# Small halves last in the matmuls of h, x2p and o, and a list schedule with other costs for transfers, the shared port and the clock

## The chip, the core and the metric

The kernel runs on one core of a Trainium2 chip, as one program. TensorE (PE) multiplies, VectorE (DVE), ScalarE (ACT) and GpSimd (POOL) work on tiles in SBUF and PSUM, and SyncE (SP) issues most transfers. The metric is the time of one execution in microseconds on the device; the median of three runs of the kernel before is 2260.31 us (2255.88 to 2264.96).

## What is computed

```python
# 4 batches, 8 heads, 768 steps, head 48
k_n = k / (norm(k) + 1e-6)
for t in range(768):
    y[t]  = q[t] @ state
    v_old = state^T k_n[t]
    state = state + beta[t] * outer(k_n[t], v[t] - v_old)
x = y as 3072 tokens of 384 numbers
# dense layer: 384 -> 2048 -> 384
h = x @ w_in;  x = (h * sigmoid(h)) @ w_out
# eight experts of 384 -> 1024 -> 384, all of them for all tokens
P = exp(x @ w_gate - max), normalised 8 times over rows and over columns
out = sum over e of P[:, e] * (relu(x @ w1[e]) @ w2[e])
```

All is float32. The matrix multiplier takes a rounded type (fp32r), so each operand of a large product is split into a large half (the rounded number, "hi") and a small half (what rounding left, "lo"). Each product is three matmuls: hi with hi, hi with lo, lo with hi.

## The kernel before

**Two phases.** Up to about 743 us of the trace the recurrence and the dense layer run side by side; from there to the end the experts run. The recurrence is done in 12 steps of 64 tokens (s = 0 to 11). For a pair of steps, `tri(j)` inverts small triangular matrices column by column on DVE (L540 to L568, the scaling of `nu` at L545, the column operations at L553 and L555). The result goes out to HBM (`rd`) and comes back in another layout (`rt`, L595), and the PE group `z` (L614) of the step waits for that. After z follow on PE r (L627), c (L646), d (L665), y (L680), s (L696), t (L713) and, after the dense layer, l (L831); all of these are narrow matmuls of 16 to 64 columns. `gkq` (L405) makes products of keys ahead of a step. On DVE, `xs` (L701) updates the state.

**The dense layer** works on 6 blocks of 512 tokens (b = 0 to 5; two steps each) and 16 slices f of the hidden size. An `h` operation of the schedule, H(b,f) below, is 9 matmuls into one PSUM bank (L740: 3 row groups k, 3 halves each), then ACT takes the sigmoid (L746), DVE multiplies (`sg`, L750), ACT rounds to the hi half of `g` (L754) and POOL subtracts to get its lo half (L758). An `x2p` operation, X(b,f), is 9 matmuls (L782) of `g` with `w_out`, into three banks `x2p_0` to `x2p_2` that gather over f. In both, the three halves of one k or one bank follow each other. In the first block the weights are split as well: ACT takes absolute values (`wt`, L873) and the hi half (L891), and DVE makes the small half `w` in seven operations (L894 to L905).

**The experts** run in 64 rounds n, in two halves of 32 (of 1536 tokens each). A round has 15 `p` operations (L1213, products of a scheme that saves multiplications; 3 matmuls each) and 12 `o` operations (L1300; 6 matmuls each, for two f; `o{n}_{j}_{i}`). DVE adds the products up (L1022, `s`) and adds `o` to `acc` (L1316); the first copies from PSUM to `s` are ACT's (`evac`, L1227). A finished sum becomes a hidden half in `hidden` (L1239): ACT takes relu into the hi half (L1244) and in place (L1246), and POOL subtracts for the lo half (L1022; tiles `room` or `h`). POOL makes the lo halves of the expert weights (`wa` and `wb`) and the sums of weights (`wraw`).

**What sets the order.** The class `Order` is a list scheduler that runs while the kernel is built. Each operation is put in with its engine, a cost in us, what it depends on (with an offset where one is given), a priority and the buffers that it takes. `emit` simulates the engines with these costs and lets each engine take, among the operations that can start soonest, the one of highest priority; the sequence that comes out is the order of instructions of each engine. The simulation has a model of the PE clock (`pe`, with TICK, PHASE and FULL), in which an operation costs 1.85 times as much where the stretch before had too few columns. An operation marked `port=True` waits for the other of DVE and POOL where that one is also marked; the sums and splits of the experts are not marked. A transfer ends at max(t + 1.5, queue) + cost. While the pipeline fills, `idle` matmuls (L1402) stand in PE's gaps.

Of the kernel before, what the change touches and what calls it, by code (L numbers as in the profile page):

```python
# [24 lines left out]
KD = DM // 128  # L25
# [18 lines left out]
HALVES = ((slice(0, 64), 1), (slice(64, 128), 2))  # L44
NEAR_PE = 0.16
# [11 lines left out]
class Order:  # L57


    QUEUES = ("SP",)  # L60
    LAT = {"PE": 0.2, "ACT": 0.16, "DVE": 0.14, "POOL": 0.1, "SP": 0.08}
# [7 lines left out]
    TICK, PHASE, FULL = 10.24 / 3, 2.63, 2000  # L69

    def add(self, engine, cost, fn, deps=(), prio=1.5, take=(), turn=None, cols=768, port=False):

        d = [x if isinstance(x, tuple) else (x, None) for x in deps]
        self.ops.append((engine, cost, fn, d, prio, take, turn, cols, port))
        return len(self.ops) - 1
# [47 lines left out]
    def pe(self, t, cost, cols):  # L123

        left = 1.0
        while left > 1e-6:
            k = int((t - self.PHASE) / self.TICK + 1 + 1e-6)
            c = cost if self.cols.get(k - 1, 0) >= self.FULL else 1.85 * cost
# [4 lines left out]

    def emit(self, idle=None):
        self.cols, busy = {}, False
# [7 lines left out]
        while any(left.values()):  # L143
            best = None
            for e, todo in left.items():
                c = []
                for i in todo[:WINDOW]:
                    r = None if wait[i] else self.ready(i, end)
                    if r is not None:
                        lane = lanes[-8] + 0.1 if e in self.QUEUES and len(lanes) >= 8 else 0.0  # L150
                        c.append((max(r, now[e], lane, port["POOL" if e == "DVE" else "DVE"] if self.ops[i][8] else 0.0), i))
# [8 lines left out]
                t, i = min((x for x in c if x[0] <= t0 + self.NEAR[e]), key=rank)  # L160
                if best is None or t < best[0]:
                    best = (t, i, e)
            t, i, e = best
# [12 lines left out]
            if e in self.QUEUES:  # L176
                now[e], queue = t + 0.5, max(t + 1.5, queue) + cost
                end[i] = queue
                lanes.append(queue)
            else:  # L180
                if e == "PE":
                    busy = busy or cols == 4608
                    now[e] = max(now[e], IDLE)
                    while idle and not busy and t > IDLE and now[e] + 0.5 < t:
                        order.append((now[e], len(order), None))
                        now[e] = self.pe(now[e], 0.107, 256)
                    t = max(t, now[e])
                    narrow = turn == 1 and cols != 150
# [4 lines left out]
                else:  # L193
                    now[e] = end[i] = t + cost
                    if self.ops[i][8]:
                        port[e] = end[i]
# [10 lines left out]
def kernel(  # L207
# [115 lines left out]
    def load(s, bp, prio):  # L323
# [5 lines left out]
        def gq(p, blk):  # L329
# [3 lines left out]
                op("SP", 0.5, lambda p=p, b=b: gq(p, b), free + [O["gd", s, bp]], prio=prio - 0.1) for p, b in HALVES]  # L333

    def load_part(s, bp, part, prio):
# [4 lines left out]
        if s and not part:  # L340

            return [(op("ACT", 0.45, adma(t(a, 0), kq[s, bp, 0, :, 0]), prio=prio), 2.3),
                    (op("ACT", 0.45, adma(t(b, 0), kq[s, bp, 1, :, 0]), prio=prio), 2.3)]
        return [op("SP", 0.42, dma(t(a, part), kq[s, bp, 0, :, part]), after, prio=prio),
                op("SP", 0.42, dma(t(b, 2 * part), kq[s, bp, 1, :, part]), after, prio=prio)]
# [19 lines left out]
    def gram_k(s, bp):  # L365
# [30 lines left out]
    def gram_kq(s, bp):  # L396
# [20 lines left out]
        q = op("PE", 1.07, lambda: pe(1), ld, prio=prio, take=["a"], turn=1, cols=1088)  # L417
        m = [op("PE", 1.07, lambda: pe(0), ld + [(q, 0.0)], prio=prio, take=["a"], turn=1, cols=1088), q]
        w = []
        for k in range(2):  # L420
# [3 lines left out]
            w.append(op("SP", 0.65, lambda k=k: put(k), [e] + ([(O["nd", s][0], -9.0)] if bp and not k else []), prio=3 - 0.1 * k))  # L424
# [1026 lines left out]
```

## Time and profile before

| what | value |
|---|---|
| median of three runs | 2260.31 us (2255.88 to 2264.96) |
| the profiled execution | 2263.14 us |
| its span in the trace | 2261.4 us |
| PE busy | 2184.4 us, 97% of the span |
| DVE, POOL, ACT busy | 78%, 68%, 45% |

The span is what the profile shows from the first to the last instruction; 1.7 us lie around it. Busy shares are means over stages with different limits, so the rows further down are read by stage: 0 to 106 us fills the pipeline, 106 to 262 us is the first dense block, 262 to 743 us the other five, 743 to 822 us the start of the experts, 1480 to 1540 us their change to the second half of the tokens. "Granted clock" is the share of full speed that TensorE had; its two levels are 2.4 and 1.2 GHz. A wait row says which engine and line sat idle until what, how long in total, how many times and the longest.

### The profile page before, as it was taken

What the parts mean: (1) busy time and instruction counts of PE and PEld (TensorE: products, weight loads), DVE (VectorE), ACT (ScalarE), POOL (GpSimd) and SP (SyncE); (2) the same over time, 40 slices, a digit from 0 to 9 for tenths busy, and PEclk for the clock granted to TensorE, in tenths of its full rate; (3) what the DMA queues carried; (4) which work ended last, traced back from release to release, by engine and by line L of the source; (5) the groups of instructions that cost most, each with busy time, mean ns of one, the idle gap of its engine ahead of it and who ended that gap; (6) DMA issues with size and microseconds to landing.
All of it is one profiled execution on the core that took longest, in us unless ns stands there. A gap on an engine that the chain in (4) does not pass through costs nothing.

```text
span 2261.4 us, 40411 instructions
## 1 busy us (share of the span) xinstructions
PE 2184.4 (97%) x15750; PEld 1928.4 (85%) x15750; DVE 1760.9 (78%) x2999; ACT 1023.8 (45%) x1766; POOL 1547.7 (68%) x1387
## 2 busy tenths in 40 slices
PE   8988799999999899999999999989999999999999
PEld 8877578788877778889998999979999999999998
DVE  7695857464725698888888888897888888888887
ACT  2443333334344445454444545455454444445453
POOL 0223344445337688888788888877888888888884
PEclk9887999998989899999999999999999999999999
DMA  9767132314140201101111111111101111111101
GB/s 266 186 201 167 56 72 66 81 52 95 40 108 11 84 29 31 40 29 36 35 36 36 33 38 29 43 47 39 42 29 36 36 36 36 36 36 30 42 29 50
DMA packets 127424, 136.79 MB, mean 60 GB/s; under 512 B 83392, under 2 KB 91328, under 8 KB 127232
## 3 DMA queue, kind: packets, MB, share of 16 engines
q1 hardware_dynamic: 124864, 133.55, 21.4%
q8 instruction: 124, 2.03, 0.4%
q10 hardware_dynamic: 2368, 0.66, 0.2%
q14 instruction: 68, 0.56, 0.1%
HBM read 108.47 MB, written 25.69 MB: 59 GB/s over the span
## 4 chain that ended last, share of the span: by engine, by line
PE 64%; POOL 13%; DVE 10%; DMA 5%; issue 4%; ACT 2%; SPq 1%; DVEq 0%; POOLq 0%; ACTq 0%
PE o L1300 25%; PE p L1213 20%; PE x2p L782 6%; PE h L740 5%; DVE s L1022 4%; POOL room L1022 3%; POOL wa L1022 3%; POOL wraw L1022 2%; POOL h L1022 2%; DMA ke<-in_kq 2%; PE d L665 1%; POOL wb L1022 1%; DMA nd<-ke 1%; DVE acc L1316 1%; PE y L680 1%
## 5 line engine op out<-in xcount | busy, mean ns | idle before, releaser
L1213 PE MATMUL p<-room,wa 128*128 128x512 f32 x2880 | 732.8, 395 | 2.6 <-DVE s L1022 2.6
L1213 PEld LDWEIGHTS p<-room,wa 128*128 128x128 f32 x2880 | 537.2, 189 | 95.6 <-issue 3.0
L1300 PE MATMUL o<-wb,room 128*128 128x384 f32 x2784 | 601.2, 337 | 10.6 <-POOL room L1022 3.0
L1022 DVE TENSOR_TENSOR s<-s,p 128x512 f32<-128x512 f32 x704 | 475.8, 683 | 167.8 <-ACT s L1227 85.1
L1300 PEld LDWEIGHTS o<-wb,room 128*128 128x128 f32 x2784 | 496.7, 188 | 34.8 <-DVE acc L1316 9.3
L1022 POOL TENSOR_TENSOR room<-s,room 128x512 fp32r<-128x512 f32 x232 | 321.0, 1384 | 222.0 <-ACT s L1246 117.0
L1316 DVE SCALAR_TENSOR_TENSOR acc<-o,pr,acc 128x384 f32<-128x384 f32 x708 | 415.7, 610 | 15.0 <-PE o L1300 12.6
L1300 PE MATMUL o<-wb,h 128*128 128x384 f32 x1824 | 416.5, 336 | 6.1 <-DVE acc L1316 3.7
L1300 PEld LDWEIGHTS o<-wb,h 128*128 128x128 f32 x1824 | 327.7, 188 | 27.7 <-DVE acc L1316 2.8
L1022 POOL TENSOR_TENSOR wa<-wraw,wa 128x640 fp32r<-128x640 f32 x189 | 322.4, 1718 | 2.5 <-ACT wa L1116 2.5
L1244 ACT ACTIVATE room<-s 128x512 fp32r<-128x512 f32 x232 | 145.7, 628 | 382.5 <-DVE s L1022 382.3
L1022 POOL TENSOR_TENSOR wraw<-wraw 128x256 f32<-128x256 f32 x378 | 275.0, 748 | 20.5 <-issue 10.7
L758 POOL TENSOR_TENSOR g<-sg,g 128x512 fp32r<-128x512 f32 x96 | 129.8, 1353 | 219.9 <-ACT g L754 206.0
L1246 ACT ACTIVATE s<-s 128x512 f32<-128x512 f32 x384 | 243.1, 633 | 12.2
L782 PE MATMUL x2p<-g,w 128*128 128x512 f32 x864 | 228.9, 412 | 15.5 <-DVE w L905 5.8
L1116 ACT ACTIVATE wa<-wraw 128x640 fp32r<-128x640 f32 x189 | 138.2, 731 | 224.4 <-POOL wraw L1022 213.6
L1022 DVE TENSOR_TENSOR s<-p,s 128x512 f32<-128x512 f32 x320 | 219.5, 686 | 16.7 <-PE p L1213 2.0
L740 PE MATMUL h<-x,w 128*128 128x512 f32 x864 | 216.9, 398 | 5.9 <-DVE w L905 4.1
L782 PEld LDWEIGHTS x2p<-g,w 128*128 128x128 f32 x864 | 165.1, 196 | 59.3 <-POOL g L758 10.7
L1022 POOL TENSOR_TENSOR h<-s,h 128x512 fp32r<-128x512 f32 x152 | 208.7, 1373 | 7.9 <-ACT s L1246 7.8
L1022 DVE TENSOR_TENSOR s<-s,s 128x512 f32<-128x512 f32 x192 | 207.3, 1080 | 2.5
L740 PEld LDWEIGHTS h<-x,w 128*128 128x128 f32 x864 | 161.6, 190 | 44.2 <-DVE w L905 5.9
(177 smaller groups left out, 2260.9 us busy)
## 6 DMA issues: line engine op xcount, KB each, us to landing
wraw<-in_w SPq DMA_DIRECT2D x126, 384.0 KB, 3.0
kv<-in_kv SPq DMA_DIRECT2D x12, 768.0 KB, 5.8
ke<-in_kq SPq DMA_DIRECT2D x40, 192.0 KB, 4.4
kqp<-in_kq SPq DMA_DIRECT2D x40, 192.0 KB, 4.0
nd<-ke SPq DMA_DIRECT2D x20, 256.0 KB, 4.1
gd<-ke SPq DMA_DIRECT2D x20, 256.0 KB, 2.8
kqp<-gd SPq DMA_DIRECT2D x40, 128.0 KB, 3.8
wr<-in_w_in SPq DMA_DIRECT2D x6, 768.0 KB, 5.8
```

Source lines behind the costliest of these rows:

```text
L665: nc.tensor.matmul(out=ps[o:o + 64, h], lhsT=rt[o:o + 64, bp, h], rhs=w[o:o + 64, h], start=True, stop=True)
L680: nc.tensor.matmul(out=ps[0:64, h], lhsT=t(slice(0, 112), 1)[:, h], rhs=x[0:112, 0, h], start=True, stop=True)
L740: nc.tensor.matmul(out=ps.rearrange("p (s t) -> p s t", s=2), lhsT=w[:, k, wl], rhs=X1[:, at, k, xl], start=n == 0, stop=n == 8)
L758: nc.gpsimd.tensor_tensor(out=g[:, 1], in0=T["sg", b, f], in1=f32(g)[:, 0], op=ALU.subtract)
L782: nc.tensor.matmul(out=T["x2p", b][j], lhsT=w[:, wl, 128 * j:128 * j + 128], rhs=g[:, gl], start=f == 0 and n == 0, stop=f == NF - 1 and n ...
L1022: e.tensor_tensor(out=out, in0=in0, in1=in1, op=o)
L1116: nc.scalar.activation(P2[key][:, :, 0], R(3 + 5 * g, 8 + 5 * g), AF.Copy)
L1213: nc.tensor.matmul(out=ps, lhsT=w[:, i, wl], rhs=x[:, xl], start=k == 0, stop=k == 2)
L1244: nc.scalar.activation(P2[key][:, 0], buf(x), AF.Relu)
L1246: op2("ACT", 0.52, lambda: nc.scalar.activation(buf(x), buf(x), AF.Relu), writes=[("s", n, x)], prio=PR_H)
L1300: nc.tensor.matmul(out=ps, lhsT=h[:, hl, 128 * i:128 * i + 128], rhs=w[:, wl], start=c == 0, stop=c == 5)
L1316: op2("DVE", 0.53, lambda A=A, pk=pk, t=t: nc.vector.scalar_tensor_tensor(out=A(), in0=P2[pk], scalar=P2["pr"][:, t, e:e + 1], in1=A(), op ...
```

## The change

1. In h and x2p, and in o, the loop over the halves goes outside, so that the matmuls with a small half come last. Of the 9 matmuls of x2p the first with w's lo half is now the fourth (it was the second) and the first with g's lo half the seventh (it was the third). Of h the first with x's lo half is the fourth (was the second), the first with w's lo half the seventh (was the third). Of the 6 of o the first with the hidden lo half is the fifth (was the third).
2. The scheduler lets these operations start before the lo half is there, by offsets LATE, SOON and REST; transfers have a cost by kind and a landing time of their own (`lands`); operations of one engine that depend on each other are 0.08 to 0.12 us apart; the clock model has other numbers (FULL, KEEP, PHASE, and all `cols`); `port` now marks POOL's operations and DVE's sums of two SBUF tiles in the experts too; ties go to what has been ready longer.
3. After the fifth product (r = 4) two engines read the same PSUM tile: DVE adds it to c1, ACT copies it to c0. ACT's copy now depends on DVE's sum, and is put in ahead of the relu of c1.

```diff
@@ Order
+PORT = True
+LATE, SOON, REST = -1.2, -0.45, -0.59
+    OWN = {"PE": 0.0, "DVE": 0.12, "ACT": 0.12, "POOL": 0.11, "SP": 0.08}
-    TICK, PHASE, FULL = 10.24 / 3, 2.63, 2000
+    TICK, PHASE, FULL, KEEP = 10.24 / 3, 2.53, 1000, 120
-                lat = 0.0 if own == engine and engine not in self.QUEUES else self.LAT[own]
+                lat = self.LAT["SP"] if self.ops[d][9] else (self.OWN if own == engine else self.LAT)[own]
-            c = cost if self.cols.get(k - 1, 0) >= self.FULL else 1.85 * cost
+            c = cost if self.fast(k) else 1.85 * cost
+            self.full[k] = self.cols.get(k - 1, 0) + self.KEEP * self.fast(k - 1) >= self.FULL
-                if best is None or t < best[0]:
-                    best = (t, i, e)
+                if best is None or (t, r) < best[:2]:
+                    best = (t, r, i, e)
-                now[e], queue = t + 0.5, max(t + 1.5, queue) + cost
+                now[e], queue = t + 0.5, max(t + (self.ops[i][9] or 2.0), queue) + cost
@@ transfers, for example those of tri
-            td.append(op("SP", 0.25, w_td, [x] + free + [(y, -9.0) for y in td], prio=7 - n if j == 0 else -4.5))
+            td.append(op("SP", 0.22, w_td, [x] + free + [(y, -9.0) for y in td], prio=7 - n if j == 0 else -4.5, lands=1.66))
@@ moe_h
-            for k in range(KD):
-                for wl, xl in ((0, 0), (0, 1), (1, 0)):
+            for wl, xl in ((0, 0), (0, 1), (1, 0)):
+                for k in range(KD):
-        x1 = [x for s in (2 * b, 2 * b + 1) for bp in range(2) for x in O["x1", s, bp]]
+        x1 = [x for s in (2 * b, 2 * b + 1) for bp in range(2) for x in (O["x1", s, bp][0], (O["x1", s, bp][1], SOON))]
-        O["g", b, f] = [h, l]
+        O["g", b, f] = [h, (l, LATE)]
@@ moe_o
-            for j in range(KD):
-                for n, (wl, gl) in enumerate(((0, 0), (1, 0), (0, 1))):
+            for n, (wl, gl) in enumerate(((0, 0), (1, 0), (0, 1))):
+                for j in range(KD):
@@ weights of the dense layer
-            O["wout" if kind else "win", f + j] = [h, x]
+            O["wout" if kind else "win", f + j] = [h, (x, SOON if kind or m == 1 else -0.85)]
@@ weights of the experts
-            l = op2("POOL", 1.54, lo, writes=[key], prio=PR_W)
+            l = op2("POOL", 1.54, lo, writes=[key], prio=PR_W, port=PORT)
@@ products
-        def evac(x, r):
+        def evac(x, r, deps=()):
-                    writes=[("s", n, x)], take=["s"] if new else [], prio=PR_A)
+                    writes=[("s", n, x)], take=["s"] if new else [], prio=PR_A,
+                    port=PORT and isinstance(a, str) and isinstance(b, str))
-            4: lambda: (add("c1", "c1", 4, ADD), hidden("c1", 0, 1), evac("c0", 4)),
+            4: lambda: (add("c1", "c1", 4, ADD), evac("c0", 4, [lastw["s", n, "c1"]]), hidden("c1", 0, 1)),
@@ outputs
-                    for f in range(2):
-                        h, w = P2["h", n, f, j], P2["wb", wn(n), f]
-                        for hl, wl in ((0, 0), (0, 1), (1, 0)):
+                    for hl, wl in ((0, 0), (0, 1), (1, 0)):
+                        for f in range(2):
+                            h, w = P2["h", n, f, j], P2["wb", wn(n), f]
-                        deps=[(P2["pe"], 0.0)], take=["m"], turn=3, cols=2304, prio=PR_O)
+                        deps=[(P2["pe"], 0.0)], late=[("h", n, f, j) for f in range(2)], take=["m"], turn=3, cols=716, prio=PR_O)
```

The order of p and o on PE in the experts stays as it was, but for the matmuls inside an o. PE's order in the dense layer is another nearly throughout. Three places follow (a number after a name counts tiles; the line numbers of after are 13 to 14 higher).

On **PE in the fifth dense block** (b = 4) before, z of step 10 stands behind X(4,12) and H(4,13):

```order
L740 MATMUL h4_13_7228<-x1_106,w24_3182 128x512 x9
L782 MATMUL x2p4_0_6889<-g4_12_7226,w24_3182 128x512 x3
L782 MATMUL x2p4_1_6890<-g4_12_7226,w24_3182 128x512 x3
L782 MATMUL x2p4_2_6891<-g4_12_7226,w24_3182 128x512 x3
L614 MATMUL z10_7258<-rt_93,td11_94 32x32 x32
L740 MATMUL h4_14_7292<-x1_106,w28_3293 128x512 x9
```

The same place of the changed kernel:

```order
L753 MATMUL h4_8_7107<-x1_106,w16_2344 128x512 x9
L795 MATMUL x2p4_0_6930<-g4_6_7104,w12_2113 128x512
L795 MATMUL x2p4_1_6931<-g4_6_7104,w12_2113 128x512
L795 MATMUL x2p4_2_6932<-g4_6_7104,w12_2113 128x512
L795 MATMUL x2p4_0_6930<-g4_6_7104,w12_2113 128x512
L795 MATMUL x2p4_1_6931<-g4_6_7104,w12_2113 128x512
L795 MATMUL x2p4_2_6932<-g4_6_7104,w12_2113 128x512
L795 MATMUL x2p4_0_6930<-g4_6_7104,w12_2113 128x512
L795 MATMUL x2p4_1_6931<-g4_6_7104,w12_2113 128x512
L795 MATMUL x2p4_2_6932<-g4_6_7104,w12_2113 128x512
L627 MATMUL z10_7140<-rt_93,td11_94 32x32 x32
```

z of step 10 now stands behind X(4,6) and H(4,8), 11 wide operations earlier (six X and five H), and x2p changes its bank at every matmul.

On **DVE in the first dense block** before, between the weight splits (`wr`, `wt`, `w`) and the state of step 2 (`xs0`); `du` and `nu` are tri's, `x1` the lo half of the dense layer's input:

```order
L905 SCALAR_TENSOR_TENSOR w16_2424<-wr4_1763 128x2x384
L750 TENSOR_TENSOR sg0_9_2595<-h0_9_2555,sg0_9_2595 128x512
L701 TENSOR_TENSOR xs0_91<-xs0_91,s2_0_2662 48x384 x2
L540 TENSOR_SCALAR du_100<-du_100 128x32
L541 RECIPROCAL du_100<-du_100 128x32
L542 TENSOR_TENSOR du_100<-bu_99,du_100 128x32
L543 TENSOR_TENSOR du_100<-du_100 128x32
L720 TENSOR_TENSOR x1_106<-t2_0_2733,x1_106 128x3x128
L510 TENSOR_REDUCE ne3_1749<-sq3_1_2739 128x8
L545 TENSOR_TENSOR nu_95<-nu_95,du_100 128x1024
```

The same place after:

```order
L918 SCALAR_TENSOR_TENSOR w16_2344<-wr4_1520 128x2x384
L907 TENSOR_SCALAR wt20_2325<-wt20_2325 128x768
L908 TENSOR_SCALAR wt20_2325<-wt20_2325 128x768
L910 SCALAR_TENSOR_TENSOR wt20_2325<-wr5_2075,wt20_2325 128x768
L912 TENSOR_SCALAR wr5_2075<-wr5_2075 128x768
L914 SCALAR_TENSOR_TENSOR wr5_2075<-wr5_2075 128x768
L916 TENSOR_SCALAR wr5_2075<-wt20_2325 128x768
L918 SCALAR_TENSOR_TENSOR w20_2560<-wr5_2075 128x6x128
L714 TENSOR_TENSOR xs0_91<-xs0_91,s2_0_2643 48x384 x2
L907 TENSOR_SCALAR wt22_2374<-wt22_2374 128x768
```

The seven operations that split `wt20` now stand ahead of the state of step 2; before, they stood 20 rows behind it, after `xs0` of step 3 too.

On **POOL in round 28 of the experts** before; `<-s3` is the lo half of c1, `<-s1` of c2, `<-s0` of c5, `<-s4` of c0, `<-s5` of c3, `<-s2` of c4:

```order
L1022 TENSOR_TENSOR room5_8405<-s3_7815,room5_8405 128x512
L1022 TENSOR_TENSOR wa2_7808<-wraw_7804,wa2_7808 128x5x128
L1022 TENSOR_TENSOR wa1_7807<-wraw_7804,wa1_7807 128x5x128
L1022 TENSOR_TENSOR h3_8422<-s1_7813,h3_8422 128x512
L1022 TENSOR_TENSOR room5_8405<-s0_7812,room5_8405 128x512
L1022 TENSOR_TENSOR wa3_7809<-wraw_7804,wa3_7809 128x5x128
L1022 TENSOR_TENSOR h0_8419<-s4_7816,h0_8419 128x512
L1022 TENSOR_TENSOR room5_8405<-s5_8423,room5_8405 128x512
L1022 TENSOR_TENSOR wb2_8398<-wraw2_7805,wb2_8398 128x384
```

The same place after:

```order
L1035 TENSOR_TENSOR room5_8462<-s3_7835,room5_8462 128x512
L1035 TENSOR_TENSOR wa2_7828<-wraw_7824,wa2_7828 128x5x128
L1035 TENSOR_TENSOR wa1_7827<-wraw_7824,wa1_7827 128x5x128
L1035 TENSOR_TENSOR h3_8447<-s1_7833,h3_8447 128x512
L1035 TENSOR_TENSOR wa3_7829<-wraw_7824,wa3_7829 128x5x128
L1035 TENSOR_TENSOR room5_8462<-s0_7832,room5_8462 128x512
L1035 TENSOR_TENSOR wb2_8474<-wraw2_7825,wb2_8474 128x384
L1035 TENSOR_TENSOR wb3_8477<-wraw2_7825,wb3_8477 128x384
L1035 TENSOR_TENSOR h0_8444<-s4_7836,h0_8444 128x512
```

A split of `wa` now stands between the lo halves of c2 and c5, and both splits of `wb` ahead of the lo half of c0. So it is in most rounds.

## Rows read from the trace of the kernel before

**Rows 1.** The page's busy times, and PE and its clock in 40 slices.

```profile
PE 2184.4 (97%) x15750; PEld 1928.4 (85%) x15750; DVE 1760.9 (78%) x2999; ACT 1023.8 (45%) x1766; POOL 1547.7 (68%) x1387
...
PE   8988799999999899999999999989999999999999
...
PEclk9887999998989899999999999999999999999999
```

**Rows 2.** Windows: length, busy us of PE, PEld, DVE, ACT, POOL; granted clock; DMA.

```profile
0.00:106.00 106.00, 95.04 (x1799) 89.78 (x1799) 71.66 (x229) 37.74 (x68) 17.99 (x27) 0.89 0.88 231
106.00:172.00 66.00, 59.59 (x721) 49.18 (x717) 60.78 (x110) 31.17 (x46) 16.85 (x14) 0.87 0.64 192
172.00:262.00 90.00, 73.94 (x1127) 59.73 (x1127) 63.61 (x132) 35.95 (x65) 30.89 (x28) 0.87 0.50 121
262.00:467.00 205.00, 197.57 (x2222) 159.48 (x2216) 120.29 (x248) 73.34 (x134) 97.90 (x99) 0.98 0.32 73
467.00:554.00 87.00, 85.48 (x838) 70.31 (x834) 49.41 (x93) 32.12 (x57) 42.19 (x40) 0.98 0.34 70
554.00:572.00 18.00, 18.00 (x287) 16.84 (x287) 9.02 (x21) 5.30 (x13) 9.04 (x11) 0.62 0.46 133
...
656.00:674.00 18.00, 17.33 (x193) 15.69 (x189) 4.23 (x10) 5.77 (x14) 3.65 (x6) 0.62 0.30 99
...
822.00:1480.00 658.00, 654.55 (x3312) 592.72 (x3311) 566.55 (x880) 325.15 (x554) 554.03 (x485) 1.00 0.11 34
```

**Rows 3.** What ended waits of h (L740), x2p (L782), o (L1300): us, times.

```profile
  DVE w L905: 10.0, 7
...
  POOL g L758: 16.5, 20
  DVE w L905: 13.3, 7
...
  DVE acc L1316: 18.0, 34
```

**Rows 4.** Waits of all engines: waiting engine and tile, releaser, us, times, longest.

```profile
DVE s L1022 <- ACT s L1227: 85.1, 60, 3.2
...
PEld x2p L782 <- POOL g L758: 10.7, 13, 1.7
...
PE x2p L782 <- POOL g L758: 5.8, 7, 1.3
```

**Rows 5.** The chain of waits in 262 to 300 us: start, us, what.

```profile
287.53 4.23 PE x2p L782 x18
291.76 8.28 PE h L740 x36
```

**Rows 6.** PE's timeline: two s groups, what follows each, then narrow before wide.

```profile
564.16 0.31 PE L696 MATMUL s<-xs,kv 64*48 64x48 f32 x1
...
565.61 0.90 PE L713 MATMUL t<-ident,y 128*128 128x128 f32 x3
...
568.09 0.24 PE L696 MATMUL s<-xs,kv 64*48 64x48 f32 x1
...
568.94 0.55 PE L713 MATMUL t<-ident,y 128*128 128x128 f32 x3
...
571.27 0.22 PE L647 MATMUL c<-xs,kqp 48*64 48x48 f32 x1
571.42 3.96 PE L740 MATMUL h<-x,w 128*128 128x512 f32 x16
```

**Rows 7.** The first dense block by timeline: DVE, and one row of ACT.

```profile
179.04 0.69 DVE L750 TENSOR_TENSOR sg<-h,sg 128x512 f32<-128x512 f32 x1 [5.76 <-ACT sg L746]
...
187.94 1.12 DVE L701 TENSOR_TENSOR xs<-xs,s 48x384 f32<-48x384 f32 x2 [4.78 <-PE s L697]
...
212.57 1.09 DVE L894 TENSOR_SCALAR wt<-wt 128x768 f32<-128x768 f32 x1
...
217.36 0.95 DVE L905 SCALAR_TENSOR_TENSOR w<-wr 128x768 fp32r<-128x768 uint32 x1
...
161.43 0.92 ACT L873 ACTIVATE wt<-wr 128x768 f32<-128x768 f32 x1
```

**Rows 8.** PE's timeline where z of step 10 starts.

```profile
628.82 1.35 PE L614 MATMUL z<-rt,td 32*32 32x32 f32 x64 [1.03 <-DMA rt<-rd]
```

**Rows 9.** One round of the experts: DVE, POOL and PE by timeline.

```profile
1183.35 0.69 DVE L1022 TENSOR_TENSOR s<-s,p 128x512 f32<-128x512 f32 x1 [1.58 <-ACT s L1227]
...
1191.03 1.29 POOL L1022 TENSOR_TENSOR h<-s,h 128x512 fp32r<-128x512 f32 x1
1195.40 1.30 POOL L1022 TENSOR_TENSOR room<-s,room 128x512 fp32r<-128x512 f32 x1 [3.08 <-ACT s L1246]
...
1197.53 0.69 PE L1300 MATMUL o<-wb,h 128*128 128x384 f32 x3
```

**Rows 10.** The page's groups of instructions: busy us, mean ns of one, idle before.

```profile
L1022 POOL TENSOR_TENSOR wa<-wraw,wa 128x640 fp32r<-128x640 f32 x189 | 322.4, 1718 | 2.5 <-ACT wa L1116 2.5
```

More of the change, by code (lines that the diff above doesn't have):

```diff
@@ L132, in pe, with fast @@
         return t
+    def fast(self, k):
+        if k < 1:
+            return False
+        if k not in self.full:
+            self.full[k] = self.cols.get(k - 1, 0) + self.KEEP * self.fast(k - 1) >= self.FULL
+        return self.full[k]
     def emit(self, idle=None):
-        self.cols, busy = {}, False
+        self.cols, self.full, busy = {}, {}, False
         left, wait, then = {}, [len(o[3]) for o in self.ops], {}
@@ L150, in emit @@
                         lane = lanes[-8] + 0.1 if e in self.QUEUES and len(lanes) >= 8 else 0.0
-                        c.append((max(r, now[e], lane, port["POOL" if e == "DVE" else "DVE"] if self.ops[i][8] else 0.0), i))
+                        r = max(r, now[e])
+                        c.append((max(r, lane, port["POOL" if e == "DVE" else "DVE"] if self.ops[i][8] else 0.0), i, r))
                 if not c:
@@ L185, in emit @@
                         order.append((now[e], len(order), None))
-                        now[e] = self.pe(now[e], 0.107, 256)
+                        now[e] = self.pe(now[e], 0.107, 80)
                     t = max(t, now[e])
-                    narrow = turn == 1 and cols != 150
+                    narrow = cols in (520, 221, 240, 390, 480, 530)
                     if narrow != tiled:
@@ L194, in emit @@
                     now[e] = end[i] = t + cost
+                    if self.ops[i][9]:
+                        end[i] = queue = max(t + self.ops[i][9][0], queue) + self.ops[i][9][1]
                     if self.ops[i][8]:
-                        port[e] = end[i]
+                        port[e] = now[e]
             order.append((t, len(order), i))
@@ L340, in load_part @@
         if s and not part:
[L342 to L345, printed above, removed]
+            return [op("ACT", 0.45, adma(t(a, 0), kq[s, bp, 0, :, 0]), prio=prio, lands=(2.6, 0.36)),
+                    op("ACT", 0.45, adma(t(b, 0), kq[s, bp, 1, :, 0]), prio=prio, lands=(2.6, 0.36))]
+        return [op("SP", 0.36, dma(t(a, part), kq[s, bp, 0, :, part]), after, prio=prio, lands=2.3),
+                op("SP", 0.36, dma(t(b, 2 * part), kq[s, bp, 1, :, part]), after, prio=prio, lands=2.3)]
     def load_kv(s, prio):
@@ L996, with op2 @@
     last, lastw, readers, touched = NSTEP - 1, {}, {}, {}
-    def op2(engine, cost, fn, reads=(), writes=(), deps=(), **kw):
+    def op2(engine, cost, fn, reads=(), writes=(), deps=(), late=(), **kw):
         own = {"DVE": 0.13, "ACT": 0.14, "POOL": 0.1}
@@ L1003, in op2 @@
             x = lastw[k]
-            d.append((x, own.get(engine)) if sc.ops[x][0] == engine else x)
+            d.append((x, own.get(engine)) if sc.ops[x][0] == engine else (x, REST) if k in late else x)
         for k in writes:
@@ L1107, in weights @@
         for k, fn in sums:
-            x = op("POOL", 0.15 + 0.27 * k, fn, [x], prio=PR_W)
+            x = op("POOL", 0.15 + 0.27 * k, fn, [(x, 0.0)] if len(x_) > 2 else [x], prio=PR_W, port=PORT)
             x_.append(x)
@@ L1133, in weights @@
             O[key] = op2("ACT", 0.42, hi, reads=["R2"], writes=[key], take=["wb"], prio=PR_W)
-            op2("POOL", 0.98, lo, reads=["R2"], writes=[key], prio=PR_W)
+            op2("POOL", 0.98, lo, reads=["R2"], writes=[key], prio=PR_W, port=PORT)
     def tokens(m):
@@ L1247, in hidden @@
             op2("POOL", 1.25, lambda: tt("POOL", P2[key][:, 1], buf(x), f32(P2[key])[:, 0], SUB),
[L1248 removed]
+                reads=[("s", n, x)], writes=[key], prio=PR_H, port=PORT)
             drop(O["s", n, x], "s", ("s", n, x))
```

87 lines of the change are left out of this document (43 added, 44 removed).

## The prediction

> **What bounds the kernel now.** First the page: PE is busy for 97% of the span, and of the 40 slices the first twelve or so have lower digits, in PE as in its granted clock [rows 1]. So the time is PE's, and there are three ways to gain: less work (the change has none), fewer waits, and fewer stretches at the lower clock. Next the windows, which tell where those are [rows 2]. In the experts there is little: from 822 to 1480 us PE is busy for 654.55 of 658 us at full clock. Up to 262 us it idles 11 + 6.4 + 16.1 us (window less busy), and the clock is 0.87 to 0.89. Between 262 and 743 us idling is small, but two stretches of 18 us have a granted clock of 0.62. With levels of 1.2 and 2.4 GHz a mean of 0.62 over 18 us is 0.76 of it, 13.7 us, at 1.2 GHz. The same sum gives 17 and 23 us for 106 to 262, and 8 and 3.5 us for 262 to 554. What runs in the slow stretches is narrow attention work: an s group takes 1.45 us at the lower clock (564.16 to 565.61) and 0.85 at the higher (568.09 to 568.94) [rows 6]. Last the waits by line [rows 3, 4]: h and x2p wait for DVE's weight splits and POOL's lo halves, o for DVE's `acc`.
>
> **The change part by part.** A wide matmul takes 230 to 235 ns (8.28/36, 4.23/18) [rows 5], so H and X take some 2.1 us.
>
> *g's lo half last.* x2p waits for POOL's lo half 20 times, 16.5 us, 0.83 each [rows 3]. The matmul that needs it moves from third to seventh, 4 x 0.235 = 0.94 us later, so a mean wait disappears and the longest, 1.7 [rows 4], leaves 0.8. But 10.7 of the 16.5 are waits of the weight loads, which run ahead of PE; PE itself shows 5.8. The ends are 0 (the scheduler may start X earlier by what is gained) and 16.5; I take 8, near the row of PE itself. **-8.**
>
> *The first block's weights.* DVE works in its order: it sits 5.76 us before a `sg` and 4.78 before `xs` [rows 7] while `wt20`, whose absolute values ACT finished at 161.43 + 0.92 = 162.35, waits behind both until 212.57. Its seven operations last until 218.31, 5.7 us. After, they stand ahead of that `xs`, in the idle time, and all later weights can come 5.7 us earlier. Besides, the lo half of w is needed two slots later in x2p and four in h, at least 0.47 us for each of the 14 waits for it, 6.6 us. The 14 waits are 10.0 + 13.3 = 23.3 us [rows 3], the most there is to gain; the least is 0, if `xs`, now behind the split, delays step 2 by as much as the weights gain. I take 5.7 + 6.6. **-12.**
>
> *Narrow work among wide.* In the order of before I count six runs of over 4 us of narrow operations without a wide one (after the start, and with the durations of the trace at full clock), together 67 us: 17.1, 17, 15.9, 6.8, 4.9 and 4.9. In the order of after there are two, 16.8 and 10.4, 27 us. The slow stretches after 262 us, 8 + 3.5 + 13.7 + 13.7 = 39 us, cost half their length, 19.5; if that goes with the length of the runs, 19.5 x 27/67 = 7.9 is left, a gain of 11.6. Against it, 29 more changes between narrow and wide: the last narrow and the first wide matmul start 0.15 us apart (571.27 to 571.42), where wide work alone is not late; I take 0.09 of that, 2.6 us. Ends: -19.5 and +2.6 (the clock stays as it is). **-9.**
>
> *The fill.* Two groups of key products and one c move from ahead of H(0,0) to behind it, some 3 us of narrow work. It isn't gone but can fill the 6.4 us that PE idles in 106 to 172 [rows 2]. Between 0 and -3. **-2.**
>
> *ACT's copy behind DVE's sum.* DVE waits for ACT's copy of the fifth product 60 times, 85.1 us, 1.4 each [rows 4], for example before 1183.35 [rows 9]. That wait goes. It costs nothing of itself, because DVE has time; what it can give back are o's waits for `acc`, 18.0 us in 34 times [rows 3], most of which lie in the two halves' starts or behind p, where DVE's queue is late for other reasons too. ACT now waits instead, with the relu of c1 beside it; its queue is 45% busy [rows 1]. Ends 0 and -18; a third. **-6.**
>
> *z pulled forward.* A new exposure: z of step 10 stands 11 wide operations earlier, z of step 8 three (by order). z waits for the transfer `rt`, and that of step 10 came last before: PE waited 1.03 us for it [rows 8]. So if tri(5) ended no earlier against the wide work, PE would wait 11 x 2.1 + 3 x 2.1 = 29 us. But tri's columns now stand in packs of up to 17 between two `sg` (up to 10 before), and DVE has the room: 49.41 of 87 us are busy from 467 to 554 [rows 2]. I take a fifth. **+6.**
>
> The other moves (places of y, t, l among wide work, matmuls in o with f alternating, transfer costs) change what the simulation believes, not what an instruction costs: 0, covered by the same PE work.
>
> **Sum.** -8 - 12 - 9 - 2 - 6 + 6 = -31. From the profiled execution, 2263.1, this gives 2232; the median of three lies 2.8 lower, so 2229 by it. I say **2230**.
>
> **Rivals.** *The waits for rt come in full.* Tri is a chain: 62 column operations on DVE with a sum between, and it may not get shorter by packing. Then the +6 becomes +29, the time 2253, and with a gap of that length the clock falls and narrow work behind it runs at 1.45 against 0.85 us, an estimate of 4 us more for one pair of steps: **2257**. For it: z of step 10 was the last to be served already [rows 8]. Against: DVE's idle 38 of 87 us.
>
> *POOL comes late in each round of the experts.* This is the case of slower. POOL finishes the lo half of c2 at 1192.32 and waits 3.08 us for ACT before that of c5 [rows 9]; after, a split of `wa` stands between, 1.72 us [rows 10]. It fits with 1.36 us to spare. The lo half of c5 is there at 1196.70; o, which starts at 1197.53, needs it at its sixth matmul, five times 0.17 later, 1198.40 (before as after: f = 1 kept that slot). So 1.7 more. It decides from the point where the split starts over 3.06 us behind the lo half of c2, because ACT's hi half of `wa` comes late or the buffer does; from there each us is paid by PE in each of the 62 or so rounds. One us late: 2230 + 62 = **2292**. For it: the scheduler's `port` rule makes POOL's operations wait for sums of DVE in its simulation, so it places them by times that may not be true. Against: 3.06 us of cover, and POOL 68% busy [rows 1].
>
> *x2p loses the clock.* x2p now changes its bank at each of its 9 matmuls. If PE idled a little at each change and fell to 1.2 GHz for x2p, 96 x 9 x 0.235 us would be added, 203: **2433**. In the trace, 36 matmuls of h with a change at each ninth take 230 ns each [rows 5], no more than x2p's 235 with a change at each third, and the clock in that window is 0.98 [rows 2]; a change at every matmul isn't shown. The Trainium skill, "TensorE: Matmul & The Clock Gate", section "A second HAM failure mode: psum-queue depth-cycling", tells of a kernel that cycles through banks, idles a little between groups and swings between the two clock levels. By that rule this rival would be the forecast; the trace so far speaks against it.
>
> **How the numbers follow.** A measurement of this kernel can tell about 0.5% from no change, 11 us: faster is below 2249, slower above 2272. The forecast has 0.74, nearly all of it below 2249; below 2204 (all ends of the gains but one third) I leave 0.05. The rt rival has 0.15, most of it between 2249 and 2260; POOL's has 0.08, and x2p's clock 0.03. Faster 0.75, same 0.14, slower 0.11. The range of 8 in 10 reaches from 2204 to 2260: 0.69 of the forecast and 0.11 of the rt rival.
>
> **What would show it.** In the profile of the changed kernel: waits of x2p for POOL's g below 5 us (16.5 before); waits for w in h and x2p below 12 (23.3), and the last weight split before 257 us; no stretch of 18 us at 0.62 in 540 to 680 us, or one; DVE's 85.1 us behind ACT's copy gone and o's waits for `acc` at 12 or less; z's waits for rt below 8 us. I am wrong on z if that wait is 15 us or more, on POOL if o shows a wait for the lo half (`room`, `h`) of over 20 us from 822 us on, on x2p if its matmuls are over 260 ns apart. If all gains come up to 743 us but the whole is less than 20 us faster, they were given back at the start of the experts, where DVE is busy.

## The result and the profile after

| | before | after |
|---|---|---|
| median of the runs | 2258.10 us (4 runs) | 2237.74 us (4 runs, 2235.09 to 2240.93) |
| ratio | | 0.9907, 95% interval 0.9878 to 0.9935 |
| profiled execution, span | 2263.14, 2261.4 us | 2235.09, 2233.3 us |

The kernel became 20 us faster. The two profiled executions lie 28 us apart: the one of before is 5 us above its median, that of after 2.6 below. What follows by place in the trace adds up to these 28.

The page of after, as [rows 1]:

```profile
PE 2165.2 (97%) x15794; PEld 1916.8 (86%) x15794; DVE 1730.5 (77%) x2999; ACT 1035.3 (46%) x1766; POOL 1539.3 (69%) x1387
...
PE   8999799999999899999999999989999999999999
...
PEclk9799899999999999999999999999999999999999
```

PE's busy time fell by 19 us with the same matmuls (44 more idle ones in the fill): an engine at the lower clock counts as busy for longer, as the s group of [rows 6] did with 1.45 us for 0.85. PE's idle time, span less busy, fell by 9 us, from 77.0 to 68.1. The windows tell where, as [rows 2] with the same columns:

```profile
172.00:262.00 90.00, 77.59 (x1311) 63.96 (x1310) 68.66 (x137) 38.83 (x71) 31.52 (x28) 0.91 0.59 147
262.00:467.00 205.00, 197.75 (x2195) 159.82 (x2194) 128.94 (x259) 75.06 (x142) 105.45 (x101) 0.98 0.35 77
...
554.00:572.00 18.00, 16.84 (x99) 13.62 (x96) 13.90 (x29) 4.20 (x8) 7.58 (x7) 1.00 0.29 88
...
656.00:674.00 18.00, 16.51 (x73) 13.29 (x72) 11.07 (x10) 7.75 (x14) 15.95 (x13) 1.00 0.25 97
```

Both stretches of 18 us that had 0.62 have 1.00. Windows cut the two kernels at different work, though, so I compare by the same work. Each column of the next table is the start of the first matmul of an operation in the timeline of PE, less the time that all PE operations ahead of it would take at full clock without a wait (among them H and X 2.045, p 0.694, o 1.04, z and r 1.13, y 1.07, d 1.06, c 1.03, s 0.85, t 0.45, l 1.26 us, each the lower quartile of its distances from start to next start). What is left is time lost to waits, to idling and to the lower clock. The table gives it by stage: from H(0,0) to H(1,0) is "block 0", and so on to the first p of round 0; then rounds 0 to 3, 4 to 29, 30 to 33 (where the tokens change) and the rest.

| lost us | fill | block 0 | 1 to 3 | 4 | 5 | rounds 0-3 | 4-29 | 30-33 | rest | sum |
|---|---|---|---|---|---|---|---|---|---|---|
| before | 61.3 | 48.1 | 31.4 | 11.3 | 8.7 | 20.3 | 8.8 | 10.1 | 5.2 | 205.2 |
| after | 64.6 | 36.5 | 25.4 | 5.1 | 4.9 | 19.7 | 3.8 | 14.1 | 3.0 | 177.1 |
| difference | +3.3 | -11.6 | -6.0 | -6.2 | -3.8 | -0.6 | -5.0 | +4.0 | -2.2 | -28.1 |

So 24 of the 28 us come up to the first product: the first p starts at 743.44 before and at 719.12 after (PE's timeline of after):

```profile
719.12 2.21 PE L1226 MATMUL p<-room,wa 128*128 128x512 f32 x9
```

How much of this is idle time and how much the clock, the windows of these stages tell: block 0, then blocks 1 to 5, first before, then after.

```profile
106.12:262.46 156.34, 133.88 (x1854) 109.25 (x1850) 124.85 (x242) 67.00 (x111) 47.74 (x42) 0.87 0.56 151
262.46:743.44 480.98, 462.67 (x4574) 378.74 (x4571) 262.85 (x487) 177.96 (x322) 235.20 (x223) 0.96 0.27 65
```

```profile
107.54:254.17 146.63, 128.82 (x1916) 104.98 (x1914) 117.62 (x224) 64.67 (x111) 48.15 (x42) 0.91 0.61 162
254.17:719.12 464.95, 452.49 (x4570) 366.61 (x4571) 260.33 (x490) 175.61 (x322) 241.98 (x222) 0.98 0.28 65
```

PE's idle time (length less busy) fell by 4.7 us in block 0 and by 5.9 in blocks 1 to 5. By the prediction's sum on the two levels, some 41 and 38 us ran at 1.2 GHz before and some 26 and 19 after. These 34 us cost half their length, some 17 us, an estimate, since the clock is given to two places. Idle time and clock together make up the 27.6 us that the table shows for blocks 0 to 5, and the clock is the larger part.

The waits of after, by line (us, times), h first, then x2p, then o, as [rows 3]:

```profile
  DVE sg L763: 8.0, 5
  ACT w L904: 4.4, 4
...
  DVE w L918: 3.4, 5
...
  DVE w L918: 9.8, 5
  POOL g L771: 8.2, 13
...
  ACT w L904: 6.0, 2
...
  DVE acc L1330: 6.2, 5
```

x2p waits half as long for g's lo half (16.5 before), h and x2p together 13.2 us for DVE's half of w (23.3), and o 6.2 for `acc` (18.0). But other waits grew: h and x2p wait 10.4 us for ACT's half of w (4.9 before), and h 8.0 for `sg` (2.0). All waits listed for h and x2p come to 55.5 us before and 59.2 after. DVE's wait for ACT's copy, 85.1 us in [rows 4], is

```profile
DVE s L1035 <- ACT s L1240: 23.3, 27, 2.8
```

z of step 10, which waited 1.03 us in [rows 8], starts 38 us earlier without a wait, between two groups of x2p:

```profile
588.58 2.20 PE L795 MATMUL x2p<-g,w 128*128 128x512 f32 x9
590.71 1.33 PE L627 MATMUL z<-rt,td 32*32 32x32 f32 x64
591.97 2.33 PE L795 MATMUL x2p<-g,w 128*128 128x512 f32 x9
```

That was possible because tri(5) became shorter. Its scaling at the start and at the end in DVE's timeline, after:

```profile
524.09 1.22 DVE L559 TENSOR_TENSOR nu<-nu,du 128x1024 f32<-128x1024 f32 x1
...
581.70 1.23 DVE L582 TENSOR_TENSOR tu<-tu,du 128x1024 f32<-128x1024 f32 x1
```

and before:

```profile
535.58 1.21 DVE L545 TENSOR_TENSOR nu<-nu,du 128x1024 f32<-128x1024 f32 x1
...
618.93 1.22 DVE L568 TENSOR_TENSOR tu<-tu,du 128x1024 f32<-128x1024 f32 x1
```

That is 57.6 us for 83.4: its 62 short operations stand in larger packs, with nine `sg` among them where there were 14. The rows of x2p also show that a bank change at every matmul costs nothing here: nine last 2.33 us, and before, with a change at every third:

```profile
546.29 2.34 PE L782 MATMUL x2p<-g,w 128*128 128x512 f32 x9
```

### The profile page after: what moved, and what is told of

It is laid out like the page before. It is cut to its first block, busy times and chain, and to the rows that moved or that the text cites. A ratio compares the mean times of both kernels' runs of the same rounds, so it can differ in the third digit from the quotient of the medians.

```text
span 2233.3 us, 40423 instructions
## 1 busy us (share of the span) xinstructions
PE 2165.2 (97%) x15794; PEld 1916.8 (86%) x15794; DVE 1730.5 (77%) x2999; ACT 1035.3 (46%) x1766; POOL 1539.3 (69%) x1387
## 4 chain that ended last, share of the span: by engine, by line
PE 62%; DVE 3%; issue 1%; POOL 1%; ACT 1%; POOLq 0%; DVEq 0%; ACTq 0%
PE o L1314 34%; PE p L1226 28%; DVE s L1035 2%; DVE room L1035 1%; DVE acc L1330 0%; POOL room L1035 0%; POOL pr L1374 0%; ACT room L1258 0%; DVE sm L1379 0%; POOL wa L1035 0%; DVE acc L1035 0%; ACT s L1260 0%; DVE sm L1387 0%; DVE xraw L1035 0%; ACT acc L1322 0%
## 5 line engine op out<-in xcount | busy, mean ns | idle before, releaser
L1314 PE MATMUL o<-wb,room 128*128 128x384 f32 x2784 | 794.5, 338 | 4.7 <-POOL room L1035 2.2
L1314 PE MATMUL o<-wb,h 128*128 128x384 f32 x1824 | 610.7, 337 | 5.7 <-DVE acc L1035 2.9
L1314 PEld LDWEIGHTS o<-wb,room 128*128 128x128 f32 x2784 | 514.6, 189 | 27.7 <-POOL room L1035 3.5
L1330 DVE SCALAR_TENSOR_TENSOR acc<-o,pr,acc 128x384 f32<-128x384 f32 x708 | 432.9, 614 | 93.9 <-PE o L1314 87.6
L1314 PEld LDWEIGHTS o<-wb,h 128*128 128x128 f32 x1824 | 343.2, 188 | 20.2 <-issue 3.6
L1035 POOL TENSOR_TENSOR room<-s,room 128x512 fp32r<-128x512 f32 x232 | 302.4, 1308 | 82.4 <-ACT s L1260 80.5
L753 PE MATMUL h<-x,w 128*128 128x512 f32 x864 | 219.0, 402 | 10.4 <-DVE sg L763 5.5
L1258 ACT ACTIVATE h<-s 128x512 fp32r<-128x512 f32 x152 | 95.3, 627 | 178.5 <-DVE s L1035 178.4
```

The costliest lines, as they stand in the source:

```text
L753: nc.tensor.matmul(out=ps.rearrange("p (s t) -> p s t", s=2), lhsT=w[:, k, wl], rhs=X1[:, at, k, xl], start=n == 0, stop=n == 8)
L1035: e.tensor_tensor(out=out, in0=in0, in1=in1, op=o)
L1258: nc.scalar.activation(P2[key][:, 0], buf(x), AF.Relu)
L1314: nc.tensor.matmul(out=ps, lhsT=h[:, hl, 128 * i:128 * i + 128], rhs=w[:, wl], start=c == 0, stop=c == 5)
L1330: op2("DVE", 0.53, lambda A=A, pk=pk, t=t: nc.vector.scalar_tensor_tensor(out=A(), in0=P2[pk], scalar=P2["pr"][:, t, e:e + 1], in1=A(), op ...
```

## Experiments

All ratios are to the kernel before, run beside them; the changed kernel has 0.9907. On 2260 us 0.001 is 2.3 us. A loss of 0.002 to 0.003 is within the two intervals (0.9878 to 0.9935 for the changed kernel), so where a part is undone I also compare the times themselves: those of the changed kernel lie between 2235.09 and 2240.93 us.

### The loops alone, and all but the loops

```diff
@@ the kernel before: h, x2p and o as in the change, nothing else
-            for k in range(KD):
-                for wl, xl in ((0, 0), (0, 1), (1, 0)):
+            for wl, xl in ((0, 0), (0, 1), (1, 0)):
+                for k in range(KD):
```

> The kernel before with the three loops of h, x2p and o turned (small halves last) and nothing else: every engine keeps the order of before. By the prediction's sum the loops are worth 8 us (g's lo half) and 6.6 us (the later slots of w): 14.6 us, so 2243 to 2246 us, with x2p's waits for POOL's g at 5 us or less (16.5 before). First rival, the waits only change their place, since PE then meets the next late operation: 2255 to 2261. Second rival, the loops are the whole change: 2236 to 2240.

Ratio 0.9988 (0.9972 to 1.0004), 2260.46 us: nothing. And yet the waits fell as foretold; x2p's are

```profile
  DVE w L905: 6.8, 6
...
  POOL g L758: 3.2, 6
```

3.2 us for 16.5. The first rival holds: PE's idle time as a whole is 75.9 us for 77.0. By the table's method the losses are 32.5 us in blocks 1 to 3 and 14.2 in block 4 (31.4 and 11.3 before): PE reaches the next late thing sooner. One such thing is ACT's half of w, for which h waited 1.8 us before:

```profile
  ACT w L891: 7.0, 7
  DVE w L905: 4.1, 6
```

The others are narrow work in a row, at the lower clock, and z (PE z waits 4.7 us for rt, 3.7 before).

```diff
@@ the changed kernel: h, x2p and o as before
-            for n, (wl, gl) in enumerate(((0, 0), (1, 0), (0, 1))):
-                for j in range(KD):
+            for j in range(KD):
+                for n, (wl, gl) in enumerate(((0, 0), (1, 0), (0, 1))):
```

> The changed kernel with the old loops in h, x2p and o, its schedule kept. The schedule lets X start up to 1.2 us before g's lo half is there; with the old loops x2p needs it at the third matmul, 0.47 us in. By the prediction the 14.6 us come back, and some more because X is placed for it: 2252 to 2262 us, with x2p's waits for POOL's g above 20 us. First rival, the loops give nothing and the order everything: 2236 to 2241.

Ratio 0.9934 (0.9915 to 0.9954), 2247.49 us: some 6 us of the gain are lost (0.0027), less than the low end of my range of 2252. The intervals overlap, the times do not (2246.70 to 2252.49). x2p's waits rise:

```profile
  POOL g L771: 24.6, 35
  DVE w L918: 12.5, 7
```

24.6 us for 8.2, PE idles 77.6 us in all for 68.1, and blocks 1 to 3 lose 33.0 us for 25.4. So the loops are worth something with the new order and nothing with the old one.

```diff
@@ the changed kernel
-LATE, SOON, REST = -1.2, -0.45, -0.59
+LATE, SOON, REST = None, None, None
-            O["wout" if kind else "win", f + j] = [h, (x, SOON if kind or m == 1 else -0.85)]
+            O["wout" if kind else "win", f + j] = [h, (x, None)]
```

> The changed kernel with the new loops, but the scheduler told to wait for the lo halves in full (LATE, SOON and REST off). Turning the loops alone gave nothing (2260.5 against 2260.5) and turning them back 6 us or so; so a theory is that the gain of the loops is in starting operations earlier, by these offsets. Then 2244 to 2250 us. Rival, the gain is in the slots themselves, and the offsets only reshuffle: 2236 to 2242.

Ratio 0.9906 (0.9877 to 0.9936), 2238.67 us. The theory falls: the offsets themselves are worth nothing that can be measured. The slots matter because the halves are late on the chip, not because the scheduler was told.

### The two readers of the fifth product

```diff
@@ the changed kernel (first) and the kernel before (second)
-            4: lambda: (add("c1", "c1", 4, ADD), evac("c0", 4, [lastw["s", n, "c1"]]), hidden("c1", 0, 1)),
+            4: lambda: (add("c1", "c1", 4, ADD), hidden("c1", 0, 1), evac("c0", 4)),
...
-            4: lambda: (add("c1", "c1", 4, ADD), hidden("c1", 0, 1), evac("c0", 4)),
+            4: lambda: (add("c1", "c1", 4, ADD), evac("c0", 4, [lastw["s", n, "c1"]]), hidden("c1", 0, 1)),
```

> The changed kernel with ACT's copy of the fifth product as it was (no order behind DVE's sum; put in behind the relu of c1). The prediction gave the order of the two readers 6 us, by o's waits for acc; the two traces differ by 3.8 us from the first product to the end. So 2241 to 2244 us, with DVE waiting some 60 to 85 us for ACT's copy again and o's waits for DVE's acc above 12 us (6.2 now). Rival, DVE has the time and the order of the two is free: 2236 to 2239.

> The kernel before with ACT's copy of the fifth product behind DVE's sum and nothing else (the order of the experts shifts with it a little). By the prediction's term 2251 to 2254 us (2258 before), with DVE's wait for ACT's copy far below 85 us and o's waits for acc at 12 us or less (18.0 before). Rival, free: 2256 to 2260.

Undone: 0.9930 (0.9910 to 0.9950), 2248.61 us, some 5 us of the gain (0.0023) and more than I expected; the times (2243.87 to 2250.43) do not overlap with the changed kernel's. Alone: 0.9992 (0.9977 to 1.0007), 2259.66 us, nothing measurable, although DVE's wait went there too and o's waits for `acc` fell to 12.3 us. Its trace does lose only 4.4 us in rounds 4 to 29 (8.8 before), but 4.6 more than before in block 0 and 3.0 more where the tokens change. The waits of the first, then of the second:

```profile
DVE s L1035 <- ACT s L1240: 54.8, 67, 3.2
...
PEld o L1314 <- POOL room L1035: 16.5, 22, 1.4
...
PE o L1314 <- POOL room L1035: 9.2, 22, 1.0
```

```profile
DVE s L1022 <- ACT s L1227: 11.3, 15, 2.8
```

The loss is not where I looked for it. In the changed kernel without the order of the two readers, o waits for POOL's lo half (22 times up to 1.4 us), not for `acc`: rounds 4 to 29 lose 11.9 us for 3.8. It is not the prediction's rival, in which a split of `wa` keeps POOL busy. In rounds 4 to 29 POOL stood idle ahead of each of these lo halves; one of them, with what it waited for:

```profile
888.75 0.63 ACT L1258 ACTIVATE room<-s 128x512 fp32r<-128x512 f32 x1 [2.82 <-DVE s L1035]
...
890.13 1.29 POOL L1035 TENSOR_TENSOR room<-s,room 128x512 fp32r<-128x512 f32 x1 [2.56 <-ACT s L1260]
```

POOL waits for ACT, and ACT for a sum of DVE, which works without a break from 881 us until then. So it is DVE's sum that comes late. How ACT's copy, a few products earlier, puts it there is not shown.

### Where narrow work stands

```diff
@@ the changed kernel
+    for s, b, f in ((8, 3, 12), (10, 4, 13)):
+        sc.ops[O["z1", s]][3].append((O["h", b, f], 0.0))
     sc.emit(idle)
```

> The changed kernel with z of step 8 held behind H(3,12) and z of step 10 behind H(4,13), where they stood before; the scheduler orders the rest anew. The prediction gave the mixing of narrow and wide work 9 us, and feared 6 us for z pulled forward; the trace of the changed kernel shows no wait of z for rt, and 6.6 us gained between H(4,8) and H(5,0). If the tail of steps 10 and 11 is the reason: 2243 to 2250 us (2239 for the changed kernel on this scale), with a run of narrow work and a stretch at the lower clock near 640 to 670 us. Rival, the place of z is free, because the wide work lost there is found elsewhere: 2236 to 2241.

Ratio 0.9927 (0.9899 to 0.9955), 2244.33 us, inside what I expected; the interval reaches below the changed kernel's ratio, and the times (2240.40 to 2252.29) touch its own, so the trace has to carry it. Narrow work without a wide matmul, in runs of over 4 us from 262 us to the first p, lasts 60 us in the trace of before, 11.7 after, and 44 here, at 539 and at 635 us. In the trace of before the two longest run from 549 to 572 and from 645 to 669 us, where its stretches at 0.62 lie. The windows of 540 to 680 us, before, after and here:

```profile
540.00:680.00 140.00, 134.77 (x1601) 114.46 (x1600) 71.27 (x136) 52.44 (x99) 56.41 (x58) 0.90 0.30 80
```

```profile
540.00:680.00 140.00, 135.83 (x1428) 111.08 (x1425) 65.77 (x117) 56.32 (x107) 72.96 (x69) 0.99 0.27 76
```

```profile
540.00:680.00 140.00, 135.11 (x1535) 114.47 (x1530) 64.39 (x118) 53.09 (x101) 64.15 (x60) 0.91 0.30 81
```

PE is as busy in all three; the granted clock is 0.90, 0.99, 0.91. Blocks 4 and 5 lose 8.5 and 8.6 us (5.1 and 4.9 after).

### The first block's weights

```diff
@@ the changed kernel
+        O["split", n] = xs_[1]
...
+    for n in (20, 22):
+        sc.ops[O["split", n]][3].append((O["sa", 3, 0], None))
     sc.emit(idle)
```

> The changed kernel with the split of wt20 and wt22 held behind xs of step 3, where it stood before; the rest is ordered anew. The prediction gave 5.7 us to the earlier split. So 2243 to 2247 us, with H(1,0) some 5 us later than 254.2 us and more waits of h and x2p for w. Rival, the first block waits for the attention steps anyway, and the split is hidden: 2236 to 2241.

Ratio 0.9853 (0.9826 to 0.9881), 2227.48 us: faster by some 11 us than the changed kernel. Neither theory had that. By stage:

| lost us | fill | block 0 | 1 to 3 | 4 | 5 | rounds 0-3 | 4-29 | 30-33 | rest | sum |
|---|---|---|---|---|---|---|---|---|---|---|
| after | 64.6 | 36.5 | 25.4 | 5.1 | 4.9 | 19.7 | 3.8 | 14.1 | 3.0 | 177.1 |
| split held back | 62.9 | 44.1 | 19.4 | 3.5 | 4.3 | 15.5 | 3.8 | 11.6 | 3.0 | 168.1 |
| the same, no port | 63.3 | 44.6 | 20.6 | 3.5 | 5.3 | 21.6 | 3.0 | 13.5 | 3.5 | 178.9 |

In block 0 the theory is right: 7.6 us are lost. But blocks 1 to 5 give 8.2 back, so at the first p it is 2.2 us ahead, 716.91 against 719.12, 1.7 of which are the fill's. H(0,10) starts at 187.3 us in the changed kernel and at 221.6 here; why the later blocks win it back is not shown. The other 6.7 us are in the experts' start and change, where the piece that was moved is not. To see whether they are its own:

```diff
@@ the kernel with the split held back
-PORT = True
+PORT = False
```

> The changed kernel with the split of wt20 and wt22 held back (2227.5 alone) and PORT off (2235.6 alone, 2239 for the changed kernel). If both are true effects of separate places, phase one and the experts, they add: 2222 to 2226 us, the fastest so far. If they are not: 2227 to 2235.

Ratio 0.9902 (0.9885 to 0.9919), 2237.15 us. PE's order is the same as in the kernel before it up to the first p, and so are the losses there within 3 us; rounds 0 to 3 lose 21.6 us for 15.5. The windows of these four rounds, with PORT and without:

```profile
716.92:816.40 99.48, 89.03 (x441) 77.25 (x439) 81.07 (x164) 50.43 (x93) 80.13 (x81) 0.98 0.19 64
```

```profile
720.00:825.54 105.54, 94.13 (x440) 81.18 (x439) 84.76 (x166) 50.02 (x92) 78.87 (x81) 0.94 0.18 60
```

PE idles about as long (10.5 and 11.4 us); what differs is its busy time, 5.1 us, at a granted clock of 0.98 and 0.94. So over half of the 11 us lie in the experts' start of that one kernel, most of that in its clock. PORT off in the changed kernel:

> The changed kernel with PORT off: POOL's operations and DVE's sums of two SBUF tiles in the experts are not kept apart in the simulation. PE's order is the same but for a few places; POOL, ACT and DVE change theirs in the experts. The prediction gave this part nothing: 2236 to 2241 us. Rival: it is what keeps POOL's lo halves in time in the experts, where 3.8 us were gained: 2242 to 2246 us.

Ratio 0.9885 (0.9857 to 0.9913), 2235.56 us: no difference from 0.9907 that can be told, and the expected rival falls. With PORT off, holding the split back changes 0.9885 to 0.9902, with it on 0.9907 to 0.9853. So holding it back gains only with PORT on.

### The models of the clock and of transfers, and a control

```diff
@@ the changed kernel: old clock model; then one landing time; then the control
-    TICK, PHASE, FULL, KEEP = 10.24 / 3, 2.53, 1000, 120
+    TICK, PHASE, FULL, KEEP = 10.24 / 3, 2.63, 2000, 0
...
+        cols = self.COLS[cols]
...
-                now[e], queue = t + 0.5, max(t + (self.ops[i][9] or 2.0), queue) + cost
+                now[e], queue = t + 0.5, max(t + 1.5, queue) + cost
...
-        g = op("DVE", 0.62, mul, [e], prio=18)
+        g = op("DVE", 0.66, mul, [e], prio=18)
```

> The changed kernel with the scheduler's model of the clock put back (PHASE, FULL, no KEEP, the columns of before); the rest, loops, offsets, transfers and copy, as changed. Theory: the new model is what makes narrow and wide work mix, and its share is that of the tails, so this goes the way of the run that held z back (2244): 2243 to 2250 us, with longer runs of narrow work and a stretch at the lower clock in the tails. Rival: the costs of transfers moved z, and the clock model is free: 2236 to 2242.

> The changed kernel with one landing time (1.5 us) for every transfer of SyncE's queue in the simulation, as before the change; costs by kind stay. Theory: z was moved forward because the scheduler now knows when rt lands; without it z goes back and PE waits or the narrow work bunches: 2243 to 2250 us. Rival: 2236 to 2242.

> A control: the changed kernel with one cost in the simulation, that of DVE's sg, at 0.66 for 0.62 us. Nothing of the change is undone, but PE's order differs in 52 places up to the experts. If single reorderings of this kind carry no time, 2236 to 2242 us (2239 for the changed kernel), and the 11 us that holding the split back gained are a true effect. If orders scatter by themselves, the time lies 5 us or more off, to either side, and no verdict of a few us on one moved piece can be put down to that piece.

The control has 0.9897 (0.9876 to 0.9917), 2237.49 us: 52 pieces of another order move the time by nothing, though the stages scatter (block 5 loses 10.7 us for 4.9, blocks 1 to 3 22.3 for 25.4). So single stages of a trace scatter by some 6 us, totals by less. The granted clock of the whole span scatters too, from 0.973 to 0.984 in 11 executions of the kernel before, so the clock of a stretch in one trace is one draw.

The old clock model has 0.9932 (0.9914 to 0.9950), 2243.97 us, some 6 us lost, as expected; the times (2242.57 to 2249.67) do not overlap with the changed kernel's. Blocks 1 to 3 lose 30.8 us and block 5 10.5; the narrow runs after 262 us come to 22 us.

One landing time costs most, as much as a theory of z and bunching gave at its upper end and more: 0.9970 (0.9954 to 0.9987), 2254.94 us, 14 us of the gain (0.0063). Its twelve runs lie between 2242.90 and 2260.86 us, and the profiled one is the fastest of them. So the trace shows a part: PE waits for the keys that gkq needs, mostly in the first block, where the changed kernel hardly does, and blocks 0 and 4 lose 45.3 and 12.0 us (36.5 and 5.1). Some 6 us were won ahead of that, since H(0,0) starts at 101.61 us for 107.54. Of its waits over the whole span:

```profile
PE gkq L418 <- DMA ke<-in_kq: 8.7, 5, 4.3
...
PE z L627 <- DMA rt<-rd: 3.7, 2, 2.3
```

What the other eleven add is not in a trace.

## Why the prediction was right, and where its steps were not

I said 2230 us in 2204 to 2260; measured were 2237.74, 20 us less than before where I had 31. The sum is nearer than its terms. Three of them took 26 us from waits (8, 12 and 6), one gave 6 back and one took 9 from the clock; in the trace PE idles 9 us less in all, and the clock gives some 17 up to the first product. Waits on PE were thus worth less than their length and the clock more than I had put in, and that the two errors nearly cancel is luck.

- **g's lo half last, -8.** The waits fell by 8.3 us. But the step from a shorter wait to a shorter time was wrong: the loops alone removed 13.3 us of that wait and gave nothing. They are worth about 6 us only with the new order. In the changed kernel other waits took their place, those for ACT's half of w and for `sg`. The least I gave, 0, was for another reason (the scheduler starting X earlier), and the run without offsets shows that this plays no part.
- **The first block's weights, -12.** Block 0 lost 11.6 us less, and the waits for DVE's half of w fell from 23.3 to 13.2. That the sizes agree is in part chance: PE's idle time there fell by 4.7 us, and the rest is the granted clock, 0.91 for 0.87, which I had not put there. I put the seven operations at 5.7 us, and holding them back costs block 0 7.6. What failed is that I carried the gain to the end. Blocks 1 to 5 take it back, and the whole kernel is not slower with the split held back.
- **Narrow work among wide, -9.** Blocks 4 and 5 lost 10.0 us less, and both slow stretches went. Holding z back alone costs 0.0020, 4.5 us, with an interval that overlaps, and in the trace the 0.91 comes back. For these two blocks the size was right, as far as the runs can tell; what I left out is that block 0 gains clock too.
- **The fill, -2.** H(0,0) starts 1.4 us later instead, with 3.3 us more lost ahead of it. I had looked at what stands just ahead of H(0,0), not at the earlier part: z of step 0 starts at 66.61 us, 2.98 later than before.
- **ACT's copy, -6.** The experts lost 3.8 us less: 5.0 in rounds 4 to 29 and 2.2 at the end, with 4.0 given back where the tokens change, which I had not thought of. The path I named, o's waits for `acc`, shrank from 18.0 to 6.2, but the run without this part shows another, POOL's lo half behind a late sum of DVE, as above.
- **z pulled forward, +6.** Nothing: no wait for rt is left. Packing made tri(5) 26 us shorter. I had bounded this by DVE's idle time, which was the right row, and then taken the cautious fifth.
- **The rivals.** rt: no. POOL late: o waits 5.8 us for POOL's `room` in all 64 rounds together, not 62. x2p's clock: nine matmuls take 2.33 us with a bank change at each, as the 2.34 before. The rule of the Trainium skill named there ("TensorE: Matmul & The Clock Gate", "A second HAM failure mode: psum-queue depth-cycling") does not bite in this kernel, where matmul follows matmul without a gap; no run here has such gaps with bank changes.

Of my tests, x2p's wait (8.2, I said below 5) and the wait for w (13.2, below 12) missed, the last split ends at 266 us and not before 257, and DVE's wait for ACT's copy is 23.3 us and not gone; the others held. My -31 stands against -28 between the two profiled executions, from one of which I worked; the 8 us from there to -20 are that these lie on either side of their medians.

Open: why PE has the higher clock at the experts' start in the kernel with the split held back, the fastest here at 2227.48 us, and what the other runs of the kernel with one landing time wait for. The shorter gaps between operations of one engine, the rule for ties and the costs of transfers by kind were never undone, and of the scheduler's parts none was tried alone in the kernel before. The losses of the parts undone one by one (0.0027, 0.0023, 0.0025 and 0.0063) sum to more than the whole gain of 0.0093, so they are not shares of it.

## What to carry to other kernels

A wait that a trace shows on the bounding engine is worth its length only if nothing else stands ready to be late at the same place; remove it alone first, and see whether the engine's whole idle time falls with it. Where narrow and wide matmuls share PE, count the time that narrow work runs alone and read the granted clock beside it: PE is "busy" either way. When a scheduler reorders everything, run a neutral perturbation as a control before a few us are put down to one moved piece.

## What the runs showed that I had not expected

Undoing a model of the transfers inside the scheduler, not an instruction, cost the most: one landing time in place of those by kind took the ratio from 0.9907 to 0.9970. And a kernel with the same PE order up to the first product, and another order of DVE, ACT and POOL in the experts, differed by 10 us (2227.48 against 2237.15), 6 of them in the first four rounds by the traces, at a granted clock of 0.98 against 0.94.
